# Taking the first expert's first 128 rows out of the expert stage and into the last steps of attention

## The chip, the cores and the metric

The kernel runs on one core of a Trainium2 chip. The metric is the device time of one execution in microseconds (us). A matmul engine (TensorE, PE in the rows; its weight loads are PEld), a vector engine (VectorE, DVE), an activation engine (ScalarE, ACT), a general engine (GpSimd, POOL) and a queue engine that mostly starts transfers (SyncE, SP) run in parallel, each in its own program order, and wait for one another through semaphores. A name with a q behind it (PEldq, DVEq, SPq) is the sequencer of that engine.

## The reference

Three layers, one after the other:

```
scores = q @ k.T / 8            # 4 batches, 8 heads, 576 tokens, 64 wide
keep the 32 largest scores of each row, softmax over them, times v
x = heads side by side          # 2304 tokens x 512
rows with x @ w_skip > 0:  e = argmax(x @ w_gate)      # 8 experts
    x += gate * (relu(x @ w1[e]) @ w2[e])              # w1 512x1024, w2 1024x512
h = x @ w_in;  g = h * sigmoid(1.702 h);  out = g @ w_out   # 512 -> 2048 -> 512
```

All weights are given, all in float32 except w_in and w_out, which come as float64. Counted from the reference's inputs, expert 0 gets 26, 31, 48 and 26 rows in the four batches (131 in all) and expert 1 gets 62; the largest expert has 182.

## The kernel before

**Attention.** `body` runs a loop over steps n = 0, 1, 2, ... Each step holds one block of 128 query rows of one head, nine blocks to a pair of heads, 16 pairs, so NTL = 144 blocks. A block passes through some twenty small stages, each delayed by a fixed number of steps: scores on TensorE (`qk`), copy (`scopy`), search for the 32nd largest on VectorE (`cand`, `merge`, `below`, `pick`), masks on ScalarE and GpSimd (`sign`, `side`, `center`, `clip`), transposes on TensorE (`tpose`, L370 and L371), exponentials (`evac`, L359) and the product with v (`av`, L427 to L434). The lists `stages` and, from step 146, `tail` set the order in which a step's instructions enter the queues. The loop ends with n = 157; from n = 144 on no new block begins and the pipeline runs empty.

**Routing.** After each batch the gates are computed and every row gets a place in its expert's list: `rank` (matmuls), `place` (VectorE and GpSimd), `lists` (five matmuls, L703, and an addition to LST, L706). For batch 3, the last, this is the way into the next stage: `last_gate` (L547 to L553) adds the last heads' share of the gates block by block, `gating_last` and `rank` run behind the loop, then `place`, `order` (which puts the experts in order of size, expert 0 always first), `short_lists` (L716), a gather of the first expert's rows (`first_rows`, L117) and a branch (L927 reads a flag, L1008 is the branch) past code for rows that do not fit. Short runs of matmuls that compute nothing (`warm`, L259) stand around `rank`.

**Experts.** Eight experts in the order `turns`. The four largest have room for 192 rows (a tile of 128 and one of 64), the others for 128. `turn` (L1078) transposes the gathered rows, `layer1` (L1091) multiplies with w1 in plain fp32, `layer2` (L1109) multiplies with w2 split in two fp32r parts (`split_w2`, L1136 and L1137): 24 matmuls of 512 columns for a tile of 128 rows, 16 for one of 64. In the same loop SP loads w1 two experts ahead (L94; two buffers) and w2 one ahead (L104), and `split_f64` turns the float64 w_in into two fp32r parts, in 16 chunks (L1030 the load, L1033 to L1035 on VectorE, L1038 and L1039). `take(e)` starts the chunks that expert e converts after its layer 1: three for a large expert, one for a small one. The last expert's chunk is converted inside its layer 1, at f = 2. Results go back to memory by an indirect write (`scatter`, L1126).

**The last layer** is a dense loop of fp32r matmuls that ends the kernel, and no line of the change is in it.

Of the kernel before, what the change touches and what calls it, by code (L numbers as in the profile page):

```python
# [8 lines left out]
F32 = mybir.dt.float32  # L9
F32R = mybir.dt.float32r  # L10
BF16 = mybir.dt.bfloat16
I32 = mybir.dt.int32
# [17 lines left out]
def body(ctx: ExitStack, tc: tile.TileContext, q, k, v, w_skip, w_gate, w1, w2, w_in, w_out, out):  # L30
    nc = tc.nc
    V, A, G, T, SY = nc.vector, nc.scalar, nc.gpsimd, nc.tensor, nc.sync
    P = 128
# [77 lines left out]
    V.tensor_copy(own, iop)  # L111
    IX0 = cst.tile([P, 2], I32, name="IX0")
    IXG = cst.tile([P, 2], I32, name="IXG")
    ZD = dram.tile([P, 8], F32, name="ZD")

    def fetch_rows(xg, ix, src=XD):
# [4 lines left out]
    def first_rows(ready=False):  # L121
        w, src = (DM, X2D) if ready else (DM + 1, XD)
        if not ready:
            V.tensor_copy(IX0, IDX[:, :2])
            gate_places()
        fetch_rows(x0[0][:, :w], IX0[:, :1], src)
        fetch_rows(x0[1][: NS - P, :w], IX0[: NS - P, 1:], src)

    def gate_places():
        V.tensor_scalar(IXG, IX0, float(DM + 1), float(DM), op0=ALU.mult, op1=ALU.add)  # L130

    def first_gates():
        one = XD.rearrange("r (w o) -> (r w) o", o=1)
        fetch_rows(x0[0][:, DM:], IXG[:, :1], one)
        fetch_rows(x0[1][: NS - P, DM:], IXG[: NS - P, 1:], one)

    with ExitStack() as ph:
        ph.enter_context(tc.manual_schedule())
# [399 lines left out]
        def last_gate(r, u):  # L538
            b, hp = divmod(NP - 1, HP)
            xb, g = xbs[b % 2], gs_[b % 2]  # L540
            rows = P if r < 4 else 64
            if r == 0 and u == 0:
                st["lx"] = wp.tile([P, S], F32, name="z")
            xt = st["lx"][:, r * P : r * P + rows]
            zt, zg = SS[:, r * P : r * P + rows], SS[:rows, 1024 + 9 * r : 1033 + 9 * r]
            if u == 0:
                T.transpose(zt, xb[:rows, r, hp * P : (hp + 1) * P], ident[:rows, :rows])  # L547
            elif u == 1:
                V.tensor_copy(xt, zt)
            elif u == 2:  # L550
                T.matmul(zg, xt, W9[:, hp, :], start=True, stop=True)
            else:
                V.tensor_tensor(g[:rows, r, :], g[:rows, r, :], zg, op=ALU.add)  # L553
            yield
# [193 lines left out]
        def stage(f, m):  # L748
            yield from f(m) or ()
# [21 lines left out]
        G.iota(tie, pattern=[[-1, E]], base=0, channel_multiplier=0, allow_small_or_imprecise_dtypes=True)  # L771
        A.activation(tie, tie, AF.Copy, scale=1.0 / 16)
        V.memset(tie[:, :1], 1.0e6)
        place_no = xbp.tile([P, E, E], F32, name="place_no")
        G.iota(place_no, pattern=[[1, E], [0, E]], base=0, channel_multiplier=0, allow_small_or_imprecise_dtypes=True)
        expert_no = xbp.tile([1, E, E], F32, name="expert_no")
# [5 lines left out]
        by_place = least[:, : 2 * E * E].rearrange("p (a c e) -> p a c e", a=E, c=2)  # L782
        over = xbp.tile([1, E], F32, name="over")
        kept = xbp.tile([1, E, E], F32, name="kept")

        def order():
            V.tensor_tensor(rnk, base, tie, op=ALU.add)
# [64 lines left out]
        V.tensor_copy(IOF.rearrange("p (e c) -> p e c", c=2), ior[:, :LW].rearrange("p (e c) -> p e c", c=NTT)[:, :, :2])  # L852
        V.tensor_copy(WHICH, which)
        fetch_rows(x0[0][:, :8], own, ZD)
        CHECKS = [NTL + AVL - 4, NTL + AVL - 2, NTL + AVL + 3]
        for n in range(NTL + AVL + 4):
            p, i = divmod(n, 9)
# [4 lines left out]
            if n == NTL // 2:  # L862
                w1t = load_w1(0)
                raws = load_w2(0)
            live = [stage(f, n - lag) for f, lag in (tail if n >= NTL + LAST else stages) if span(f, n - lag)]
            gates = [(p - 2, i - 6) if i >= 6 else (p - 3, i + 3)]
            gates = [gu for gu in gates if 0 <= gu[0] < NP - 1]
# [9 lines left out]
            if i == 0 and "fin" in st:  # L877
                todo.append(place())
                fresh.append(todo[-1])
            elif i == 0 and "hot" in st:  # L880
                live.append(lists(1))
            live += [some(g, 3 if g in fresh or n >= NTL else 1) for g in todo]
            fresh.clear()
            while live:
                live = [g for g in live if next(g, 1) is None]
# [9 lines left out]
                    next(last_gate(r, 2 * w))  # L895
            if n in CHECKS:
                check(CHECKS.index(n))
            if i == 8 and "fin" in st:
                rank()
            elif i == 8 and "hot" in st:  # L900
                next(lists(0))
        for g in todo:
            for _ in g:
                pass
        warm(2)
        rank()
        warm(7)
        pg, og = place(), order()
        next(pg)
        next(pg)  # L910
        for w, _ in enumerate(pg):
# [4 lines left out]
            if 1 < w < 5:  # L916
                next(og, None)
        short_lists(0)
        short_lists(1)
        first_rows(True)  # L920
        for _ in og:
# [2 lines left out]
        st.pop("hot")  # L924
        sort_lists()
        gate_places()
        fine = nc.values_load(flags[:, 1:2], min_val=0, max_val=1)  # L927

        def exact(n):
# [78 lines left out]
        with tc.If(fine < 1):  # L1008
            full_lists()
            good = nc.values_load(flags[:, :1], min_val=0, max_val=1)  # L1010
            with tc.If(good < 1):
                for t in (base, LST):
                    V.memset(t, 0.0)
                with tc.For_i(0, B, 1) as bv:
                    again(bv)
            V.tensor_scalar(IDX, LST, padf, None, op0=ALU.add)
# [42 lines left out]
    with ExitStack() as ph:  # L1059
# [25 lines left out]

        def layer1(w1t, xgT, ns, step):
            hb = mp.tile([P, FC1, 2 * NS], F32R, name="hb", bufs=1)
            for f in range(FC1):
# [3 lines left out]
                A.activation(hb[:, f, :ns], ph_[:, :ns], AF.Relu)  # L1092
                for a, b in ((0, 2 * P), (P, NS))[: 1 + (ns > P)]:
                    V.scalar_tensor_tensor(hb[:, f, b : b + min(P, ns - a)], ph_[:, a : min(a + P, ns)], 0.0,  # L1094
                                           hb[:, f, a : min(a + P, ns)].bitcast(F32), op0=ALU.max, op1=ALU.subtract)
                step(f)
            return hb

# [28 lines left out]
                out=X2D, out_offset=bass.IndirectOffsetOnAxis(ap=ix, axis=0), in_=xo, in_offset=None,  # L1127
            )

        late = []  # L1130
        spare = []

        def split_w2(raws, ws, f, long):
# [11 lines left out]
                todo.append(split_f64(wt, w_in[c * P : (c + 1) * P, us], wih[:, c, us], wil[:, c, us],  # L1145
                                      SY if c or u > 2 else A))

        turns = [0, 4, 1, 5, 2, 3, 6, 7]
        slots = []
        for k in turns:  # L1150
            slots.append([(IXS[:, k, :1], P)] + ([(IXS[: NS - P, k, 1:], NS - P)] if k < BIGS else []))
        who = [0]
        for k in turns[1:]:
            who.append(nc.values_load(flags[:, 2 + E + k : 3 + E + k], engines=[mybir.EngineType.SP], min_val=0, max_val=E - 1))
        nxt = []
        xgs = x0
        nx = turn(slots[0], xgs)
        first_gates()
        def take(e):
            gs = [todo.pop(0) for _ in range(3 if turns[e] < BIGS else 1)]  # L1160
            for g in gs:
                next(g)
            return gs

        w1s = [w1t, load_w1(who[1])]
        ahead = take(0)
        nxt.append(gather(slots[1]))
        for e in range(E):
            long = turns[e] < BIGS
            ns = NS if long else P  # L1170
            ws = ([], [])

            def step(f):
# [183 lines left out]
```

## Time and profile before

| | us |
|---|---|
| three runs | 1033.44, 1039.68 (median), 1041.09 |
| profiled execution | 1033.63, its span 1030.7 |
| TensorE busy / weight loads | 989.4 / 842.9 |
| VectorE / ScalarE / GpSimd busy | 704.6 / 593.1 / 478.3 |
| mean granted TensorE clock | 0.988 of full |

A row of the view by windows gives, for a stretch in us from the span's start, the busy time of each engine, how many instructions began, the granted TensorE clock (1.00 is 2.4 GHz, 0.50 is 1.2 GHz), the busy share of the 16 transfer engines and what they moved in GB/s. The chain of waits is followed backwards from the last instruction: each line is a start, a length and what the kernel's end hung on then. A timeline line is a start, a length, engine, line, operation, tiles and count; in brackets the idle time of the engine before it and what ended that. A fp32 matmul appears as two records, a fp32r one as one.

Attention takes the span's first 455 us, the experts the stretch from 467 to 615 us, the last layer the rest.

### The profile page before, as it was taken

The numbers are of one execution on the slowest core, as the hardware profiler recorded it, in microseconds if no ns is written. First come the engines' busy times: TensorE is split into PE (matmuls) and PEld (weight loads), VectorE is DVE, ScalarE is ACT, GpSimd is POOL, SyncE is SP. The second block draws the span as 40 slices with busy tenths as digits, with TensorE's granted clock in tenths as the row PEclk, the third lists the DMA queues.
The fourth block names the chain that finished last, engine by engine and source line by source line (L and its number), as shares of the span: only waits on it lengthen the run. The fifth ranks groups of instructions, "written<-read, shape, count | busy, mean of one in ns | idle before, by whom it ended". The sixth has DMA issues, their size and how long they took to land.

```text
span 1030.7 us, 20024 instructions
## 1 busy us (share of the span) xinstructions
PE 989.4 (96%) x6499; PEld 842.9 (82%) x6499; DVE 704.6 (68%) x3326; ACT 593.1 (58%) x1261; POOL 478.3 (46%) x598
## 2 busy tenths in 40 slices
PE   7999999999999999878999989999999999999998
PEld 4888888888888888757989877888888888888887
DVE  7999999999999999965898976653232323322222
ACT  6999999999999999823534533332222222222222
POOL 5788888978898879733765652220000000000000
PEclk9999999999999999998999999999999999999999
DMA  3121116161511151037889863312000200100000
GB/s 87 44 45 38 33 37 130 40 203 40 132 40 40 40 125 24 1 95 281 276 328 385 301 218 134 102 62 73 10 1 1 82 1 1 62 1 1 9 33 21
DMA packets 99010, 92.11 MB, mean 89 GB/s; under 512 B 71760, under 2 KB 71760, under 8 KB 98896
## 3 DMA queue, kind: packets, MB, share of 16 engines
q1 hardware_dynamic: 96704, 83.91, 26.8%
q0 software_dynamic: 1760, 5.25, 1.5%
q10 hardware_dynamic: 432, 1.57, 0.4%
q8 instruction: 53, 0.87, 0.4%
q14 instruction: 61, 0.50, 0.2%
HBM read 72.38 MB, written 17.32 MB: 87 GB/s over the span
## 4 chain that ended last, share of the span: by engine, by line
PE 71%; DVE 18%; DMA 4%; ACT 3%; issue 2%; POOL 1%; another core or an unknown queue 1%; SPq 0%; DVEq 0%; ACTq 0%; POOLq 0%
PE ph L1279 19%; PE py L1264 18%; PE Y L430 7%; DVE C L296 5%; PE SS L273 5%; PE pt L370 4%; DVE z L329 2%; DMA raw<-in_moe_w_in_dram 2%; PE ph L1091 2%; PE pt L371 2%; PE SS L275 2%; PE py L1109 2%; DVE w2l L1137 1%; PE Y L427 1%; PE SS L267 1%
## 5 line engine op out<-in xcount | busy, mean ns | idle before, releaser
L296 DVE MAX8 C<-s 128x8 f32<-128x72 f32 x1152 | 222.0, 220 | 2.2 <-ACT s L289 2.2
L324 POOL TENSOR_TENSOR z<-s,z 128x576 f32<-128x576 f32 x144 | 203.3, 1412 | 43.3 <-ACT z L319 41.1
L1267 DVE TENSOR_TENSOR g<-py,g 128x512 f32<-128x512 f32 (+1 forms) x80 | 51.1, 639 | 180.1 <-ACT g L1266 180.1
L1266 ACT ACTIVATE g<-py 128x512 f32<-128x512 f32 (+1 forms) x80 | 44.3, 554 | 166.9 <-PE py L1264 166.8
L430 PE MATMUL Y<-vn,AT 128*128 128x65 f32 x1024 | 121.3, 272 | 0.0
L430 PEld LDWEIGHTS Y<-vn,AT 128*128 128x128 f32 x1024 | 119.4, 192 | 0.0
L356 ACT ACTIVATE k<-s,th 128x576 bf16<-128x576 f32 x144 | 113.4, 788 | 5.6 <-DVE T L337 5.0
L1279 PE MATMUL ph<-woh,gh 128*128 128x512 f32 x288 | 112.6, 391 | 3.3 <-ACT gh L1269 3.3
L319 ACT ACTIVATE z<-s,T 128x576 f32<-128x576 f32 x144 | 113.0, 785 | 4.0 <-DVE T L312 1.8
L370 PE MATMUL pt<-ident,a 128*128 128x128 f32 x576 | 114.6, 279 | 0.8 <-issue 0.8
L1279 PE MATMUL ph<-woh,gl 128*128 128x512 f32 x288 | 112.5, 391 | 0.0
L1279 PE MATMUL ph<-wol,gh 128*128 128x512 f32 x288 | 112.5, 391 | 0.0
L351 POOL TENSOR_SCALAR a<-s,m 128x576 f32<-128x576 f32 x144 | 108.0, 750 | 1.5
L329 DVE MAX8 z<-z 128x8 f32<-128x576 f32 x144 | 107.0, 743 | 0.2 <-POOL z L324 0.2
L371 PE MATMUL pt<-far,k 128*128 128x128 bf16 x576 | 106.1, 220 | 0.6 <-ACT k L356 0.5
L359 ACT ACTIVATE AT<-pt 128x512 f32<-128x512 f32 x144 | 86.7, 602 | 8.5 <-PE Y L430 7.2
L370 PEld LDWEIGHTS pt<-ident,a 128*128 128x128 f32 x576 | 82.9, 144 | 6.3 <-issue 1.0
L1271 DVE TENSOR_TENSOR gl<-g,gh 128x512 fp32r<-128x512 f32 (+1 forms) x80 | 51.1, 639 | 52.4 <-ACT gh L1269 48.5
L1264 PE MATMUL py<-xh,wih 128*128 128x512 f32 (+1 forms) x320 | 81.1, 375 | 0.8 <-ACT xh L1298 0.8
L1091 PE MATMUL ph<-xgT,w1t 128*128 128x192 f32 (+1 forms) x512 | 75.8, 309 | 6.1 <-DVE hb L1094 5.4
L1091 PEld LDWEIGHTS ph<-xgT,w1t 128*128 128x128 f32 x512 | 74.1, 197 | 7.8 <-DVE hb L1094 6.5
L1269 ACT ACTIVATE gh<-g 128x512 fp32r<-128x512 f32 (+1 forms) x80 | 47.1, 589 | 56.6 <-DVE g L1267 56.6
(263 smaller groups left out, 2137.1 us busy)
## 6 DMA issues: line engine op xcount, KB each, us to landing
w1t<-in_moe_w_dram SPq DMA_DIRECT2D x8, 2048.0 KB
w<-in_moe_w_dram SPq DMA_DIRECT2D x64, 256.0 KB
raw<-in_moe_w_out_dram SPq DMA_DIRECT2D x16, 512.0 KB
raw<-in_moe_w_in_dram SPq DMA_DIRECT2D x13, 512.0 KB
out_dram<-ot SPq DMA_DIRECT2D x18, 256.0 KB
qn<-in_q_dram SPq DMA_DIRECT2D x32, 128.0 KB
kn<-in_k_dram SPq DMA_DIRECT2D x32, 128.0 KB
vn<-in_v_dram SPq DMA_DIRECT2D x32, 128.0 KB
```

What stands on the lines that cost most here:

```text
L296: V.max(C[:, g, :], s[:, g * SEG : (g + 1) * SEG])
L319: A.activation(z, d["s", c], AF.Sign, bias=T24[:, NTL + 6 - n : NTL + 7 - n], scale=-1.0 - 2.0 ** -20, accum_out=sg)
L324: G.tensor_tensor(z, d["s", c], z, op=ALU.mult)
L329: V.max(z8, d.pop(("z", c)))
L351: G.tensor_scalar(a[:, o : o + S], d.pop(("s", c)), -1.0, d.pop(("m1", c))[:, :1], op0=ALU.mult, op1=ALU.add)
L356: A.activation(d["k", r][:, o : o + S], d["s", c], AF.Relu, bias=d.pop(("th", c)), scale=-1.0)
L370: T.matmul(out, a, ident, is_transpose=True, start=True, stop=False)
L371: T.matmul(out, d["k", r][:, sl], far, start=False, stop=True)
L430: T.matmul(y[:, w * j : w * j + w], t[:, 4 * j + g, :], d["v"][:, g, j, :], start=False, stop=(j == 1 and g == 3))
L1091: T.matmul(ph_[:, :ns], w1t[:, c, f * P : (f + 1) * P], xgT[:, c, :ns], start=(c == 0), stop=(c == KC - 1))
L1264: T.matmul(phh[:, :n], lh[:, c, fs], rh[:, c, :n], start=(u == 0 and c == 0), stop=(u == 2 and c == KC - 1))
L1279: T.matmul(po[t], lh[:, ts_], rh[f], start=(f == 0 and u == 0), stop=(f == FC2 - 1 and u == 2))
```

## The change

The first 128 places of expert 0 are filled from batches 0 to 2 alone: after those batches' lists, `base` of expert 0 is raised to at least 128, so that the last batch's rows begin at place 128. The rows are gathered on their own (`early_rows`), and `early_turn` computes them in plain fp32, in 20 slices that enter the queues at the end of steps 148 to 157 (table `EARLY`) and behind the loop, in place of the `warm` matmuls. After the branch expert 0 has one tile of 64 rows. The early result is added by `early_out` just ahead of the branch and is the first to be scattered.

Around this: the lists of batch 2 are made earlier (two pieces of `place` a step from step 135, and its lists as soon as `place` is through instead of at a pair's end), expert 1 is forced to the last place in the order of sizes and is always computed second, so that its w1 can be loaded in attention (step 90) instead of after the branch; `turns` and the chunks of w_in per expert (`MORE`) change; `last_gate` uses other columns of the buffer SS, whose third part the early work takes.

```diff
-        fetch_rows(x0[0][:, :w], IX0[:, :1], src)
         fetch_rows(x0[1][: NS - P, :w], IX0[: NS - P, 1:], src)
...
+        V.memset(tie[:, 1:2], -1.0e6)
...
+        def early_rows():
+            V.tensor_scalar(base[:, :1], base[:, :1], float(P), None, op0=ALU.max)
+            V.tensor_scalar(IXA, LST[:, :1], padf, None, op0=ALU.add)
+            V.tensor_scalar(IXB, LST[:, :1], padf, float((B - 1) * S - 1), op0=ALU.add, op1=ALU.min)
+            fetch_rows(x0[0], IXB, XD[: (B - 1) * S, :])
+            yield
+        EZ = SS[:, 1024:]
+        def early_turn():
+            for c in range(KC):
+                T.transpose(EZ[:, c * P : (c + 1) * P], x0[0][:, c * P : (c + 1) * P], ident)
+            yield
+            st["ex"] = sp.tile([P, 2, S], F32, name="s").rearrange("p j k -> p (j k)")
+            A.activation(st["ex"][:, :DM], EZ, AF.Copy)
+            st["eh"] = sp.tile([P, 2, S], F32, name="s").rearrange("p j k -> p (j k)")
+            yield
+            for f in range(FC1):
+                z = EZ[:, f % 4 * P : (f % 4 + 1) * P]
+                for c in range(KC):
+                    T.matmul(z, w1t[:, c, f * P : (f + 1) * P], st["ex"][:, c * P : (c + 1) * P],
+                             start=(c == 0), stop=(c == KC - 1))
+                yield
+                if f % 4 == 3:
+                    A.activation(st["eh"][:, (f - 3) * P : (f + 1) * P], EZ, AF.Relu)
+                    yield
+            for f in range(FC1):
+                T.matmul(EZ, st["eh"][:, f * P : (f + 1) * P], raws[f], start=(f == 0), stop=(f == FC1 - 1))
+                yield
+        def early_out():
+            V.scalar_tensor_tensor(x0[0][:, :DM], EZ, x0[0][:, DM:], x0[0][:, :DM], op0=ALU.mult, op1=ALU.add)
...
+        SOON = NTL - 9
+        EARLY = {4: 1, 5: 1, 6: 1, 7: 1, 8: 2, 9: 2, 10: 1, 11: 2, 12: 1, 13: 1}
...
+            if n == NTL * 5 // 8:
+                w1u = load_w1(1)
...
-            elif i == 0 and "hot" in st:
+            elif st.pop("listed", i == 0 and n < SOON and "hot" in st):
                 live.append(lists(1))
-            live += [some(g, 3 if g in fresh or n >= NTL else 1) for g in todo]
+                if n > SOON:
+                    live.append(early_rows())
+            live += [some(g, 3 if g in fresh or n >= NTL + 4 else 2 if n >= SOON else 1) for g in todo]
...
+            for _ in range(EARLY.get(n - NTL, 0)):
+                next(eg, None)
...
-        warm(2)
+        next(eg)
         rank()
-        warm(7)
+        for _ in range(4):
+            next(eg)
...
         short_lists(0)
+        for _ in eg:
+            pass
         short_lists(1)
...
         gate_places()
+        early_out()
...
-        late = []
+        late = [(IXA, x0[0][:, :DM])]
...
-        turns = [0, 4, 1, 5, 2, 3, 6, 7]
+        turns = [0, E - 1, 1, 4, 2, 3, 5, 6]
+        MORE = [1, 2, 3, 2, 3, 3, 2, 0]
...
+        slots[0] = slots[0][1:]
...
-            gs = [todo.pop(0) for _ in range(3 if turns[e] < BIGS else 1)]
+            gs = [todo.pop(0) for _ in range(MORE[e])]
...
-        w1s = [w1t, load_w1(who[1])]
+        w1s = [w1t, w1u]
...
-            long = turns[e] < BIGS
-            ns = NS if long else P
+            long = 0 < e and turns[e] < BIGS
+            ns = NS if long else P if e else NS - P
```

## Rows read from the trace of the kernel before

**Rows 1.** View by windows, stretches of 5 us: four near attention's end, one among experts.
```profile
425.00:430.00 5.00, 4.11 (x39) 3.59 (x38) 5.00 (x36) 3.65 (x10) 3.86 (x6) 1.00 0.01 3
...
440.00:445.00 5.00, 3.54 (x35) 3.28 (x33) 3.02 (x9) 2.46 (x5) 3.29 (x7) 1.00 0.01 3
445.00:450.00 5.00, 5.00 (x47) 4.63 (x46) 3.08 (x14) 1.15 (x3) 0.00 (x0) 1.00 0.00 0
450.00:455.00 5.00, 3.92 (x28) 3.17 (x28) 2.63 (x14) 0.38 (x1) 0.00 (x0) 1.00 0.65 235
...
475.00:480.00 5.00, 5.00 (x33) 5.00 (x32) 2.94 (x10) 3.20 (x9) 1.94 (x2) 1.00 1.01 384
```

**Rows 2.** The chain of waits, from the last gates to the branch.
```profile
441.66 0.39 PE SS L551 x2
...
446.67 1.73 PE Y L430 x16
...
449.90 0.51 PE Z L703 x5
...
454.45 0.30 PE SS L551 x2
...
456.13 0.21 DVE MS L617
...
459.67 0.20 DVE hc L683
...
461.59 5.57 another core or an unknown queue
```

**Rows 3.** Timeline of TensorE in the expert loop.
```profile
467.30 1.70 PE L1078 MATMUL pt<-ident,xg 128*128 128x128 f32 x8 [5.71 <-remote]
469.60 12.66 PE L1091 MATMUL ph<-xgT,w1t 128*128 128x192 f32 x64 [0.60 <-ACT xgT L1080]
...
482.45 0.48 PE L1109 MATMUL py<-w2h,hb 128*128 128x512 f32 x1
...
491.62 7.70 PE L1091 MATMUL ph<-xgT,w1t 128*128 128x128 f32 x64
...
505.65 10.56 PE L1091 MATMUL ph<-xgT,w1t 128*128 128x192 f32 x64
...
606.89 2.08 PE L1091 MATMUL ph<-xgT,w1t 128*128 128x128 f32 x8 [3.45 <-DVE hb L1094]
```

**Rows 4.** Timelines of single instructions whose like the change adds or removes.
```profile
446.19 0.60 ACT L359 ACTIVATE AT<-pt 128x512 f32<-128x512 f32 x1 [0.91 <-PE pt L371]
...
450.87 0.30 DVE L706 TENSOR_TENSOR LST<-LST,Z 128x144 f32<-128x144 f32 x1 [0.64 <-ACT xt L522]
...
462.15 1.11 POOL L117 DMA_INDIRECT xg<-X2D,IX  x1 [1.25 <-DVE kept L809]
...
463.14 0.16 DVE L130 TENSOR_SCALAR IXG<-IX 128x2 int32<-128x2 int32 x1
...
602.17 0.43 DVE L1033 TENSOR_SCALAR t<-raw 128x512 int32<-128x512 int32 x1 [1.15 <-DMA raw<-in_moe_w_in_dram]
```

**Rows 5.** Transfers into the tile xg, from issue to landing, stretch 440 to 520.
```profile
DMA to landing us min/median/max: 3.3/5.8/6.9
```

**Rows 6.** The branch's line L1008: its instructions on two sequencers (duration in ns).
```profile
L1008 PEldq COMPARE_BRANCH  x1: 4007/4007/4007, 462.0 to 462.0; - x1
...
L1008 DVEq EVENT_SEMAPHORE  x2: 21/21/21, 467.0 to 467.1; - x2
```

**Rows 7.** View by windows of 1 us; the granted clock is third from the end.
```profile
457.00:458.00 1.00, 1.00 (x4) 0.33 (x3) 0.96 (x10) 0.00 (x0) 0.14 (x1) 0.50 1.08 225
...
464.00:465.00 1.00, 0.00 (x0) 0.00 (x0) 0.00 (x0) 0.00 (x0) 0.48 (x1) 0.50 0.74 209
...
472.00:473.00 1.00, 1.00 (x5) 1.00 (x5) 0.07 (x1) 0.43 (x2) 0.00 (x0) 0.50 0.92 336
...
474.00:475.00 1.00, 1.00 (x8) 1.00 (x8) 0.14 (x1) 0.50 (x2) 0.77 (x1) 1.00 1.01 398
```

More of the change, by code (lines that the diff above doesn't have):

```diff
@@ L113, in body @@
     IXG = cst.tile([P, 2], I32, name="IXG")
+    IXA = cst.tile([P, 1], I32, name="IXA")
+    IXB = cst.tile([P, 1], I32, name="IXB")
     ZD = dram.tile([P, 8], F32, name="ZD")
@@ L132, in first_gates @@
     def first_gates():
-        one = XD.rearrange("r (w o) -> (r w) o", o=1)
-        fetch_rows(x0[0][:, DM:], IXG[:, :1], one)
-        fetch_rows(x0[1][: NS - P, DM:], IXG[: NS - P, 1:], one)
+        fetch_rows(x0[1][: NS - P, DM:], IXG[: NS - P, 1:], XD.rearrange("r (w o) -> (r w) o", o=1))
     with ExitStack() as ph:
@@ L544, in last_gate @@
             xt = st["lx"][:, r * P : r * P + rows]
-            zt, zg = SS[:, r * P : r * P + rows], SS[:rows, 1024 + 9 * r : 1033 + 9 * r]
+            z0 = r % 4 * P
+            zt, zg = SS[:, z0 : z0 + rows], SS[:rows, 512 + 9 * r : 521 + 9 * r]
             if u == 0:
@@ L897, in body @@
                 check(CHECKS.index(n))
+            for _ in range(EARLY.get(n - NTL, 0)):
+                next(eg, None)
             if i == 8 and "fin" in st:
                 rank()
-            elif i == 8 and "hot" in st:
+            elif "hot" in st and (i == 8 if n < SOON else i != 5 and "listed" not in st):
                 next(lists(0))
+                if n >= SOON:
+                    st["listed"] = True
         for g in todo:
@@ L1015, in body @@
                     again(bv)
+                V.tensor_copy(IXA, padf)
+                V.tensor_scalar(IDX, LST, padf, None, op0=ALU.add)
+                spill(0, 0)
             V.tensor_scalar(IDX, LST, padf, None, op0=ALU.add)
@@ L1087, in layer1 @@
             hb = mp.tile([P, FC1, 2 * NS], F32R, name="hb", bufs=1)
+            spans = [(0, ns, P, NS)] if ns < P else [(0, P, 0, 2 * P), (P, ns, P, NS)][: 1 + (ns > P)]
+            o = spans[0][2]
             for f in range(FC1):
@@ L1091, in layer1 @@
                     T.matmul(ph_[:, :ns], w1t[:, c, f * P : (f + 1) * P], xgT[:, c, :ns], start=(c == 0), stop=(c == KC - 1))
[L1092 to L1095, printed above, removed]
+                A.activation(hb[:, f, o : o + ns], ph_[:, :ns], AF.Relu)
+                for a, b, hi, lo in spans:
+                    V.scalar_tensor_tensor(hb[:, f, lo : lo + b - a], ph_[:, a:b], 0.0,
+                                           hb[:, f, hi : hi + b - a].bitcast(F32), op0=ALU.max, op1=ALU.subtract)
                 step(f)
@@ L1151, in body @@
             slots.append([(IXS[:, k, :1], P)] + ([(IXS[: NS - P, k, 1:], NS - P)] if k < BIGS else []))
-        who = [0]
-        for k in turns[1:]:
+        slots[0] = slots[0][1:]
+        who = [0, 1]
+        for k in turns[2:]:
             who.append(nc.values_load(flags[:, 2 + E + k : 3 + E + k], engines=[mybir.EngineType.SP], min_val=0, max_val=E - 1))
         nxt = []
-        xgs = x0
+        xgs = x0[1:]
         nx = turn(slots[0], xgs)
```

1 line of the change is left out of this document (added).

## The prediction

> **What bounds the kernel now.** I read the view by windows first: it shows which engine is full in which stretch. Up to step 147 VectorE has no pause (5.00 of 5 in 425 to 430 us) and TensorE has some. From 441.7 us it is the other way: in 445 to 450 TensorE is busy 5.00 of 5 with its weight loads at 4.63, while VectorE has 3.08 [rows 1]. The chain of waits says the same in order of time: it lies on TensorE's queue from 441.66 until the last product with v, crosses to VectorE for the last gates (454.45 to 456.34), through `rank` and `place` to the first operand of the short lists at 459.87, and then 5.57 us stand to a queue the view can't name [rows 2]. Line L1008 names it: TensorE's branch took 4.0 us, and VectorE came out of its own at 467.0 [rows 6]. After that TensorE is the bound: expert 0 fills it from 467.30 to 491.62 [rows 3]. So the change adds TensorE work in a stretch where TensorE is short of time, and takes it out of another such stretch. The forecast is the difference.
>
> **What is added ahead of the branch.** A slice of layer 1 is 4 matmuls, 8 records of 128 columns at 7.70 / 64 = 0.120 us: 0.96 us [rows 3]. A slice of layer 2 is one fp32 matmul of 512 columns, which no row shows. By columns it costs 10.56 / 64 x 512 / 192 = 0.44 us a record, 0.88 a slice; from the step between 128 and 192 columns it is 0.40 and 0.79 [rows 3]. I take 0.87, near the first, since the pace there is set by columns. In the order of the queue:
>
> - The transposes (step 148) and their copy by ScalarE (0.60 [rows 4]) cost nothing: TensorE has 1.46 us to spare in 440 to 445 [rows 1], just ahead of 441.66, where it waits for VectorE. Without that cover: 0.7.
> - f = 0 to 3 (steps 150 to 152) stand in TensorE's queue ahead of the last two products with v: 4 x 0.96 = 3.8. The lists of batch 2, five matmuls on the chain here, leave: -0.5 [rows 2]. f = 4 writes where the relu of the first four is still reading, so TensorE waits for a copy of 0.60 [rows 4], with the last product with v queued behind it: +0.6; then itself, +1.0. Together +4.9.
> - f = 5 falls into the pause before the last gates (TensorE has 1.08 of 5 to spare in 450 to 455 [rows 1]): +0.1. f = 6 and 7 stand ahead of the last gate's matmul, 1.9 against some 0.4 of that pause: +1.5.
> - The second relu, 0.6, and two slices of layer 2, 1.7, come ahead of `rank`, beside the gating chain from the last gate to MS, 456.34 - 454.75 = 1.6 [rows 2]: +0.7.
> - Four more slices, 3.5, lie between `rank` and the short lists, where VectorE takes until 459.87 [rows 2]: nothing, if the clock is full. The last two, 1.7, run in the branch's wait.
> - `early_out` stands in VectorE's queue ahead of its branch and waits for those two slices; TensorE waits for VectorE's way out of the branch [rows 6]. I take +0.5, between 0 (the sequencers run ahead) and 2.3 (two slices and a pass like the copy of 0.60, if all queue up), nearer to the first, as TensorE's branch began at 462.0, right behind the last list matmul's end at 461.59 [rows 2, 6]. The gather of 128 rows that leaves (POOL, 1.11 [rows 4]) gives nothing back: the smaller one has its place and the branch outlasts it. The Trainium skill, Runtime: NRT & Kernel Launch, section Instruction fetch mechanics, says that a taken branch out of the fetched pages stalls its engine for a fetch; by that rule the 4.0 us begin only once the queue has come to the branch, and the sum would be up to 1.2 us higher. The trace agrees as to the 4.0 us [rows 6]; where they begin behind queued matmuls it doesn't show.
> - VectorE gets three small operations of 0.16 and the addition to LST, 0.30, earlier [rows 4], all where it is full: +0.8. The other work of `place` moves by a few steps within that stretch: nothing. GpSimd's gather, 1.1, meets an engine with 1.1 of 5 idle [rows 1]; without that cover 1.1. It lands within 6.9 us [rows 5], issued near 430 and wanted near 439.
>
> Sum: 4.9 + 0.1 + 1.5 + 0.7 + 0.5 + 0.8 = **+8.5 us**, bounds 3 to 12.
>
> **What leaves behind the branch.** Before, 24.3 us pass from 467.30 to 491.62. After: one set of transposes and one copy of the two, 1.3 instead of 2.3 [rows 3]. Layer 1 with 64 columns: its nearest rows are the 65-column records of L430, 1.73 / 16 = 0.108 [rows 2], so 64 x 0.108 = 6.9. The clock is at 1.2 GHz after the wait, 0.50 from 464 to 473 and 1.00 at 474 [rows 7]; that cost layer 1 12.66 - 10.56 = 2.1 us [rows 3], and I leave it: 9.0 (6.9 if the clock holds, 10.5 if weights load at half pace as well). Next expert's transposes 0.2. Layer 2: 16 matmuls instead of 40 at (491.62 - 482.45) / 40 = 0.229: 3.7. Together 14.2: **-10.1**.
>
> The last expert no longer converts a chunk. Before, that chunk's wait for its load (1.15 on VectorE at 602.17 [rows 4]) stopped TensorE for 3.45 at 606.89 [rows 3]. Now the expert before it has two chunks, which delays its successor's first relu by some 0.4: **-3.0**. The second and fourth experts get a second chunk too; with transfers full (1.01 at 475 to 480 [rows 1]) I take **+0.5**, bounds 0 to 7. The load of w1, 2 MB, that moves into attention is issued in step 90, seven steps ahead of SP's next transfers, and costs nothing; without that cover up to a step, 455 / 158 = 2.9.
>
> Sum: 8.5 - 10.1 - 3.0 + 0.5 = **-4.1 us**. The profiled execution, 1033.6, would become 1029.5. The median run lies 6.1 above it; the mean of the three is 1038.1, and from that I say **1034**.
>
> **The rivals.**
>
> *The early slices find more room than I count.* From 440 to 455 weight loads leave 1.72 + 0.37 + 1.83 = 3.9 of 15 us free [rows 1]; if the slices used all of it, f = 0 to 7 (7.7) would cost 7.7 - 3.9 - 0.5 = 3.3 instead of 6.5: -7.3, 1031. If the clock also held after the branch, -9.4, 1029. Against it: the records of L430 follow each other at 0.108 us, without pause [rows 2]. The Trainium skill, Perfetto Trace Analysis, section Identifying the Most-Contended Engine, says that matmul busy time is a poor measure and weight-load busy share the better one; by that rule 445 to 450 is 93% full rather than 100%, and the first figure above is its sum. The trace agrees for that stretch within 0.4 us; whether the other room can be used it doesn't show. Chance 0.20.
>
> *Slower: the second chunk stops TensorE.* In the second, fourth and seventh expert a chunk more stands in VectorE's queue ahead of the next expert's relu. Where its load lands after the layer 2 it hides behind, TensorE stops as at 606.89. Price: 3 x 3.45 = 10.4 in place of 0.5: +5.8, 1044. It decides where the second load of a pair lands later than the layer 2 in which it hides, 24 x 0.229 = 5.5 us. For it: transfers are full from 475 on; against: w1's 2 MB less are asked for. Chance 0.13.
>
> *The clock is low in the late slices.* At 457 it was 0.50 [rows 7], after a stretch with pauses. At 1.2 GHz the slices around `rank` cost 1.7 + 3.5 + 1.7 more: +2.8, 1041. Against: the slices fill those very pauses. Chance 0.10.
>
> *It doesn't do what it says*, because rows don't fit: expert 0 has 105 rows in three batches and 26 in the last, against 128 and 64, and expert 1 has 62 against 128. Excluded but for oversights: 0.02.
>
> **How the numbers follow.** The forecast as summed, between -9 and +3, has 0.55. About 1%, 10.4 us, is what a measurement can tell from no change. Beyond it on the fast side lie 0.10 of the forecast, 0.11 of the first rival, 0.01 of the rest: 0.22. On the slow side 0.02, 0.06, 0.03 and 0.01: 0.12. Within: 0.66. The range runs from -10.4 on the fastest run to a little over +2 on the slowest: 1023 to 1043.
>
> **What would show it.** Right: `rank` near 464 instead of 456.4; TensorE without pause from 441 to there; 14 to 15 us between the first transposes after the branch and the second expert's layer 1; no stop in the last expert's layer 1; a clock of 1.00 up to the branch. Wrong: `rank` before 461 (the slices found room), stops of over 1 us in the third, fifth or eighth expert, or a late landing of the early rows, which would hold TensorE's whole queue from step 148.

## The result and the profile after

The changed kernel takes 1046.7 us in the median of 11 runs (1043.7 to 1050.4), the kernel before 1035.7 in as many beside it: ratio 1.0101, 95% interval 1.0072 to 1.0129. It is slower by 1%, some 10.5 us, where I had forecast 4 us faster. The profiled execution took 1045.8 us, its span 1043.9.

The starts of a few instructions cut the spans into stages. Beside before and after stands a kernel from the experiments below, the changed one with a single line moved (f2_after_gather, here f2); its trace has the same mean clock as that of before, 0.988, while that of the changed kernel has 0.978. Block 143 is the last block of attention; a block is taken at the start of its MAX8 over 576 columns on VectorE. What I call the restart is the first transposes behind the branch.

| stage, us | before | after | f2 | forecast for after |
|---|---|---|---|---|
| start to block 133 | 411.7 | 413.9 | 413.2 | 411.7 |
| block 133 to block 143 | 29.0 | 31.7 | 29.7 | 29.8 |
| block 143 to `rank` | 15.7 | 26.2 | 25.2 | 22.9 |
| `rank` to the restart | 10.9 | 11.0 | 10.8 | 11.4 |
| expert 0 | 24.3 | 20.3 | 20.1 | 14.2 |
| second expert | 14.0 | 17.4 | 13.6 | - |
| third expert's layer 1 to the end | 525.1 | 523.4 | 519.8 | - |
| the last two together | 539.1 | 540.8 | 533.4 | 536.6 |
| span | 1030.7 | 1043.9 | 1032.4 | 1026.6 |

The timeline of TensorE after answers to [rows 3]:

```profile
471.81 0.25 PE L634 MATMUL Z<-MS,upper 128*128 128x48 bf16 x1
...
482.86 0.43 PE L1130 MATMUL pt<-ident,xg 64*128 64x64 f32 x4 [3.96 <-DVEq L1057]
483.97 13.91 PE L1145 MATMUL ph<-xgT,w1t 128*128 128x64 f32 x64 [0.67 <-DVE xgT L1134]
497.68 1.06 PE L1130 MATMUL pt<-ident,xg 128*128 128x128 f32 x4
...
503.16 7.31 PE L1145 MATMUL ph<-xgT,w1t 128*128 128x128 f32 x64
511.94 0.63 PE L1130 MATMUL pt<-ident,xg 128*128 128x128 f32 x4 [1.47 <-DMA xg<-XD,IXS]
...
568.15 1.33 PE L1130 MATMUL pt<-ident,xg 128*128 128x128 f32 x8 [2.84 <-DMA xg<-XD,IXS]
...
618.99 3.86 PE L1145 MATMUL ph<-xgT,w1t 128*128 128x128 f32 x32 [1.24 <-DVE hb L1148]
```

Three things are to be seen. Expert 0's layer 1, with 64 columns, takes 13.91 us, more than the 12.66 it took with 192. TensorE then stops at the transposes of the third expert's gathered rows, for 1.47 us, and at 568.15 at those of the sixth, for 2.84. The list of TensorE's waits (us in all, times, longest) has 4.7 us of them in place of 0.8. The last expert's stop has shrunk from 3.45 to 1.24. Before, and after:

```profile
PE pt L1078 <- DMA xg<-XD,IXS: 0.8, 2, 0.4
```

```profile
PE pt L1130 <- DMA xg<-XD,IXS: 4.7, 3, 2.8
...
PE ph L1145 <- DVE hb L1148: 1.2, 1, 1.2
```

The windows after, as in [rows 1] and [rows 7]:

```profile
428.00:436.00 8.00, 8.00 (x48) 7.34 (x47) 6.87 (x46) 5.74 (x15) 4.32 (x4) 0.57 0.13 35
...
450.00:455.00 5.00, 5.00 (x49) 4.92 (x47) 2.31 (x9) 0.84 (x2) 0.00 (x0) 1.00 0.00 0
...
484.00:500.00 16.00, 16.00 (x72) 15.71 (x73) 5.18 (x14) 5.93 (x16) 7.62 (x7) 0.50 0.62 173
513.00:518.00 5.00, 5.00 (x18) 3.91 (x19) 4.90 (x13) 0.74 (x2) 0.00 (x0) 0.66 0.78 235
```

Throughout expert 0's layer 1 the clock is at 0.50, and behind the stop at 511.94 it has fallen again. The chain of waits of this trace has no piece ahead of 600 us, so nothing answers to [rows 2].

Why the rows come late stands on GpSimd's queue. After:

```profile
497.03 1.27 POOL L1191 TENSOR_TENSOR w2l<-w,w2h 128x512 fp32r<-128x512 f32 x1 [2.15 <-ACT w2h L1190]
502.52 1.28 POOL L1091 TENSOR_TENSOR wil<-t,wih 128x512 fp32r<-128x512 f32 x1 [4.22 <-ACT wih L1090]
503.95 0.98 POOL L119 DMA_INDIRECT xg<-XD,IXS  x1
505.24 1.00 POOL L119 DMA_INDIRECT xg<-XD,IXS  x1 [0.30 <-issue]
```

And VectorE's instructions that this subtraction waits for:

```profile
499.30 0.68 DVE L1134 COPY xgT<-pt 128x512 f32<-128x512 f32 x1
499.90 0.42 DVE L1085 TENSOR_SCALAR t<-raw 128x512 int32<-128x512 int32 x1
500.36 0.69 DVE L1086 SCALAR_TENSOR_TENSOR t<-raw,t 128x512 int32<-128x512 int32 x1
501.08 0.69 DVE L1087 SCALAR_TENSOR_TENSOR t<-raw,t 128x512 int32<-128x512 int32 x1
```

The gather of the next expert but one (L119) is queued behind the chunk of w_in that an expert converts. GpSimd stands idle for 4.22 us before that chunk's subtraction, and the rows land up to 7.9 us after their issue (3.6/4.1/7.9 are the least, median and most of the tile's landings from 478 to 520 us, in place of [rows 5]).

So a chain begins at the end of expert 0's layer 1 that a faster layer 1 does not shorten: transposes and copy (497.88 to 499.98), conversion on VectorE (to 501.77), ScalarE and GpSimd (to 503.80), then the gathers, the first issued at 503.95 and landed at 511.9: 14.0 us. Beside it TensorE has layer 2 and the next layer 1. Before, that was 499.16 - 482.26 = 16.9 us, from the end of layer 1 to the third expert's transposes, which began without a stop. TensorE and GpSimd before:

```profile
499.16 0.99 PE L1078 MATMUL pt<-ident,xg 128*128 128x128 f32 x8
```

```profile
493.96 1.46 POOL L117 DMA_INDIRECT xg<-XD,IXS  x1 [0.15 <-issue]
495.72 1.29 POOL L117 DMA_INDIRECT xg<-XD,IXS  x1 [0.30 <-issue]
```

Behind three chunks the second gather left 13.5 us after the end of layer 1. With the least landing of [rows 5], 3.3, that makes an estimate of 16.8 us for this chain: it was nearly level with TensorE, and the 0.8 us of waits, two of 0.41 at the fifth and the sixth expert, say the same of the later ones. The change takes 24 of 40 matmuls out of expert 0's layer 2 and only two chunks out of the chain. With TensorE's part at full clock, 0.4 + 16 x 0.23 + 7.3 = 11.4 us, a stop of some 2.6 would have followed however fast layer 1 had become.

### The profile page after: what moved, and what is told of

The parts are those of the page before. It is cut to its first block, busy times and chain, and to the rows that moved or that the text cites. A ratio compares the mean times of both kernels' runs of the same rounds, so it can differ in the third digit from the quotient of the medians.

```text
span 1043.9 us, 20094 instructions
## 1 busy us (share of the span) xinstructions
PE 1005.3 (96%) x6546; PEld 853.4 (82%) x6546; DVE 700.6 (67%) x3321; ACT 593.8 (57%) x1263; POOL 476.6 (46%) x598
## 5 line engine op out<-in xcount | busy, mean ns | idle before, releaser
L369 PE MATMUL pt<-ident,a 128*128 128x128 f32 x576 | 116.9, 283 | 0.0
L370 PE MATMUL pt<-far,k 128*128 128x128 bf16 x576 | 108.2, 222 | 0.5 <-ACT k L355 0.3
L358 ACT ACTIVATE AT<-pt 128x512 f32<-128x512 f32 x144 | 86.7, 602 | 11.6 <-PE Y L429 7.3
L1320 PE MATMUL py<-xh,wil 128*128 128x512 f32 (+1 forms) x320 | 78.9, 368 | 0.0
L1320 PE MATMUL py<-xl,wih 128*128 128x512 f32 (+1 forms) x320 | 78.8, 368 | 0.0
## 6 DMA issues: line engine op xcount, KB each, us to landing
raw<-in_moe_w_in_dram SPq DMA_DIRECT2D x13, 512.0 KB, 10.9
```

The lines of the kernel that those rows point to most:

```text
L358: A.activation(o, i, AF.Exp, scale=-UNSC)
L369: T.matmul(out, a, ident, is_transpose=True, start=True, stop=False)
L370: T.matmul(out, d["k", r][:, sl], far, start=False, stop=True)
L1320: T.matmul(phh[:, :n], lh[:, c, fs], rh[:, c, :n], start=(u == 0 and c == 0), stop=(u == 2 and c == KC - 1))
```

## The experiments

**Does the narrow layer 1 keep the clock low, or the wait at the branch? (e1_wide)**

```diff
                     V.tensor_copy(xgT[:, :, :rows], pt[:, :, :rows])
+                    if rows < P:
+                        A.activation(xgT[:, :, rows : 2 * rows], pt[:, :, :rows], AF.Copy)
```

(That is in `turn`; in the matmul of `layer1` the columns `: ns` become `: max(ns, P)`.)

> The changed kernel, with expert 0's 64 remaining rows put twice side by side, so that its layer 1 behind the branch runs 128 columns instead of 64 (the second half is not used). Theory: the 64-column layer 1, whose matmuls are as short as the loads of their weights, leaves TensorE at 1.2 GHz; with 128 columns the clock comes back within some 7 us of the restart, as it did in the kernel before, and the 64 records take about 64 x 0.120 + 2.1 = 9.8 us, at most 11, instead of 13.9: 3 to 4 us off the changed kernel's time although there are twice the columns. Rival: the clock is low because of the idle wait at the branch, whatever the width; the 64 records then stand at the half-clock pitch all the way, 13.7 us or more, and nothing is gained. Second rival: it is no clock matter, the loads of weights alone set 0.214 us a record; then also 13.7 or more, with the granted clock at 1.00 in that stretch.

Measured: 1.0069 (1.0036 to 1.0102; such figures are the ratio to the kernel before and its 95% interval). That is 3.3 us below the changed kernel, in the theory's 3 to 4, though the two intervals overlap. Layer 1 with twice the columns took 9.45 us instead of 13.91. Its windows:

```profile
480.00:482.00 2.00, 2.00 (x9) 2.00 (x10) 0.00 (x0) 0.00 (x0) 0.80 (x1) 0.50 0.49 88
482.00:484.00 2.00, 2.00 (x11) 2.00 (x10) 0.23 (x1) 0.92 (x4) 1.06 (x1) 0.50 0.77 295
484.00:486.00 2.00, 2.00 (x18) 2.00 (x18) 1.07 (x3) 1.39 (x5) 1.38 (x3) 0.92 0.17 64
486.00:488.00 2.00, 2.00 (x20) 2.00 (x20) 1.39 (x4) 1.70 (x6) 1.49 (x2) 1.00 0.77 290
...
506.00:514.00 8.00, 8.00 (x27) 6.31 (x27) 5.99 (x10) 1.65 (x3) 2.58 (x2) 0.65 0.96 310
```

At the restart, at 478.25, the clock has fallen to 0.50, and 7 us later it is back. Only the columns differ, so the wait at the branch alone did not keep the clock low; and the second rival wanted 1.00 where the changed kernel has 0.50 (484 to 500 us above). But in this trace the second expert takes 21.0 us instead of 17.4: TensorE waits 2.9 us for the third expert's rows and then works at a low clock (506 to 514). From the restart to the end the kernel needs 561.9 us, and the changed one needs 561.0. In the traces, then, what the faster layer 1 gave was lost one expert later; the 3.3 us by the runs these stages do not show.

**Is it the early pacing? (e2_pace)**

```diff
-            live += [some(g, 3 if g in fresh or n >= NTL else 1) for g in todo]
+            live += [some(g, 3 if g in fresh or n >= NTL + 4 else 2 if n >= SOON else 1) for g in todo]
...
```

(That is in the kernel before; the lists of batch 2 come as soon as `place` is through.)

> The kernel before with nothing but the changed pacing: place and the lists of batch 2 are begun and stepped earlier in attention's last nine steps; no early rows, no slices, the old order of experts. Theory: the pacing alone, by putting VectorE's work into steps where VectorE is full, stops TensorE near step 139 and lets its clock fall, and costs some 3 us up to step 143, less the five list matmuls that leave the end (0.5): ratio about 1.002 to 1.003, the MAX8 of block 143 near 444 instead of 440.7 us, and a granted clock under 0.9 in some window between 424 and 436. Rival: the pacing is free and the early gather and its three small operations stop TensorE there: ratio 1.000, block 143 at 440.7, clock as before.

Measured: 1.0009 (0.9977 to 1.0042), which decides between neither. Its trace has block 143 at 446.0 and the clock at 0.50 from 428 to 436. But the paced kernels whose clock is full there (e1, e7 and f2) take only 0.7 us more than before between blocks 133 and 143. I put pacing and early gather together at that.

**The order of the experts alone (e3_order)**

```diff
+        V.memset(tie[:, 1:2], -1.0e6)
+            if n == NTL * 5 // 8:
+                w1u = load_w1(1)
-        turns = [0, 4, 1, 5, 2, 3, 6, 7]
+        turns = [0, E - 1, 1, 4, 2, 3, 5, 6]
+        MORE = [1, 2, 3, 2, 3, 3, 2, 0]
```

> The kernel before with nothing but the changed order behind the branch: expert 1 put last in rank and second in turn, its w1 loaded during attention, the order of sizes and the number of chunks split in each expert (1, 2, 3, 2, 3, 3, 2, 0) as in the changed kernel; expert 0 whole behind the branch, nothing early. Theory (as forecast): the last expert's stop of 3.45 goes and the extra chunks cost 0.5: -3 us, ratio 0.997. Rival: the extra chunks, the transfers that they ask for and the gathers behind them stop TensorE in the second and fifth expert, as the changed kernel's trace has it (1.5 and 3.2 us): +1 to +3 us, ratio 1.001 to 1.003.

Measured: 0.9977 (0.9950 to 1.0005), -2.4 us: near the theory's number, though not parted from no change. The rival's mechanism is in the trace as well: 3.4 us of waits for gathered rows in place of 0.8, against 3.8 us less of waits for relu, the last expert's above all. Its trace shows one thing more, told under the hardware below.

**The early slices (e4_noslices)**

```diff
-        EARLY = {4: 1, 5: 1, 6: 1, 7: 1, 8: 2, 9: 2, 10: 1, 11: 2, 12: 1, 13: 1}
+        EARLY = {}
...
```

(`warm(2)` and `warm(7)` stand around `rank` again, and `early_out` is gone: the first 128 rows of expert 0 get no expert output.)

> The changed kernel without the early expert work (its 20 slices of transposes, layer 1 and layer 2 and the addition at the end are left out, so the first 128 rows of expert 0 get no expert output), with the filler matmuls around rank put back; early gather, pacing, order and the 64-row expert 0 stay. Theory: the slices cost some 10 us between step 143 and rank and nothing else; rank comes at 456.4 + 3.3 (pacing) = 459.7, and expert 0 behind the branch is no shorter than with them, some 20 us, as the clock stays at 1.2 GHz there all the same: 10 us off the changed kernel, ratio about 1.000. Rival: the slices in the branch's wait are what keeps the clock low behind it, or what is late at the restart; without them expert 0 takes 14 to 15 us as forecast and the ratio is about 0.994.

Measured: 0.9942 (0.9908 to 0.9976). Expert 0 was no shorter, 20.6 us with the clock at 0.50 through its layer 1, as the theory had it; but the ratio is the rival's. By the runs leaving the slices out is worth some 16 us, against 10.5 between block 143 and `rank` in the traces. The profiled run here was its slowest of ten (1038.5, median 1031.7), with block 143 only at 448.0, so its stages can't tell where the other 5 come from. That stays open.

**Work in the branch's wait (e5_bridge, e6_before_bridge)**

```diff
         for _ in eg:
             pass
+        warm(18)
         short_lists(1)
```

(This is e5, filler matmuls in the changed kernel; e6 puts `warm(24)` at the same place in the kernel before.)

> The changed kernel with 18 filler matmuls of 512 columns behind the last slice of layer 2, so that TensorE has work during the branch (18 x 0.21 = 3.9 us at full clock, against 3.9 us from the last slice to the restart). It tells whether 64-column matmuls can hold a clock that is up already, where e1_wide showed that 128 columns raise one that is down. Theory A (64 columns neither raise nor hold it): the clock is at 1.00 at the restart, falls within layer 1, and layer 1 takes 11 to 13.9 us; ratio 1.007 to 1.010. Theory B (they can't raise it but hold it): layer 1 at 1.00 throughout, 64 x 0.108 = 7 us instead of 13.9, expert 0 in 13 to 14 us instead of 20.3; but the third expert's rows, whose gather waits on GpSimd behind a chunk's subtraction, come no earlier than about 26 us after the restart, and so only some 3 of the 6 to 7 us show in the total: ratio about 1.007. If the filler ran at half clock it would last 7.7 us and delay the restart by 3.8.

> The kernel before with 24 filler matmuls of 512 columns behind the list matmuls, 24 x 0.21 = 5.0 us at full clock against the 5.7 us of the branch. Theory: the clock is at 1.00 at the restart, expert 0's transposes and layer 1 take 1.5 and 10.6 us instead of 2.3 and 12.7, and the second expert's layer 1 comes 2 to 3 us earlier after the restart; the third expert's gather lands then about as late as TensorE wants it, which takes back up to 2: -1 to -3 us, ratio 0.997 to 0.999. Rival: the clock at the list matmuls is low more often than not, the filler lasts up to 10 us and the restart is up to 4 us late: ratio 1.001 to 1.003.

e5: 1.0138 (1.0121 to 1.0155), slower than either theory had it; the profiled run was its fastest of five (1042.0, median 1048.5), so the trace does not tell why. The clock was up at the restart, at 480.67, and fell all the same:

```profile
480.00:482.00 2.00, 0.66 (x6) 0.55 (x7) 0.42 (x1) 0.00 (x0) 1.70 (x2) 1.00 0.27 72
482.00:484.00 2.00, 1.54 (x11) 1.51 (x11) 0.07 (x1) 0.33 (x2) 0.08 (x1) 0.69 0.81 283
484.00:496.00 12.00, 12.00 (x59) 12.00 (x59) 3.75 (x11) 5.30 (x15) 6.08 (x5) 0.50 0.52 163
```

So theory A in the trace: layer 1 with 64 columns ran at 0.50 to its end even from a full clock, 13.8 us. The fall itself can't be put down to the columns: TensorE was busy for only 0.66 of the 2 us after 480, and in e6 the clock falls behind the restart with 192 columns. e6: 0.9974 (0.9941 to 1.0007), within the theory's range but not parted from no change. In its trace the clock falls from 475 on and is back at 479 under 192 columns; the second expert's layer 1 comes 23.3 us after the restart instead of 24.3, but the restart 13.0 us after `rank` instead of 10.9.

**The gather's place (e7_gather, f2_after_gather, f1_order_gather)**, the same edit in three kernels: e1, the changed one and e3.

```diff
+            if e + 2 < E:
+                nxt.append(gather(slots[e + 2]))
             for g in convs:
                 next(g)
                 next(g)
-            if e + 2 < E:
-                nxt.append(gather(slots[e + 2]))
```

> The kernel of e1_wide (64 rows put twice, 128 columns) with one more edit: the gather of the next but one expert's rows is issued ahead of the conversion of the chunks instead of behind it, on GpSimd's queue. Theory: in e1_wide what a faster expert 0 gave was lost in the second expert, because its successor's rows were fetched behind a subtraction that waits for a chunk's load; the second expert took 21.0 us instead of 14. With the gather ahead the rows lie there in time, TensorE does not stop at the third expert's transposes (2.1 and 0.8 us in e1_wide), the clock stays up in the layer 2 that follows, the second expert takes 14 to 16 us, and the fifth expert's wait of 3.2 us goes too: 6 to 9 us off e1_wide, ratio 0.998 to 1.001. Rival: the wait is for the transfers themselves (w1 and w2 in front of the rows), and the gather, issued earlier, lands as late as before: ratio 1.006 to 1.008.

> The changed kernel with the gather ahead of the chunks and nothing else. Theory: what the gather's place costs does not depend on the columns of layer 1; as between e1_wide and e7_gather it gives back most of 9 us even though expert 0 stays at half clock: -5 to -9 us against the changed kernel, ratio 1.002 to 1.006, with no wait for gathered rows and the second expert back at 14 us. Rival: with expert 0 at half clock the rows were late by only 1.5 us at the third expert and 2.8 at the sixth, so no more than 4.7 us come back: ratio 1.006 to 1.009.

> e3_order (the kernel before with only the changed order of experts) and the gather ahead of the chunks. Theory: the order by itself was worth 2.4 us because its gathers, behind a chunk's subtraction on GpSimd, stopped TensorE for 3.4 us in all, and the clock fell after the longest of these stops; without them it gives 5 to 8 us: ratio 0.992 to 0.995, and no wait for gathered rows in TensorE's list. Rival: only the 3.4 us of TensorE's waits come back, or less, since relu and conversions on VectorE are the next bound: ratio 0.995 to 0.998.

e7: 0.9979 (0.9948 to 1.0011), 9.3 us below e1. f2: 1.0001 (0.9970 to 1.0033): the moved line alone gives back 10 us, the whole loss, more than the theory's 5 to 9 and twice the waits that it removes. f1: 0.9955 (0.9924 to 0.9986), 2.3 us below e3, which is the rival's range and within both intervals. No wait for rows is left in any of the three. GpSimd and TensorE in f2, the last line from TensorE's waits:

```profile
493.27 1.27 POOL L1191 TENSOR_TENSOR w2l<-w,w2h 128x512 fp32r<-128x512 f32 x1 [2.14 <-ACT w2h L1190]
494.69 0.99 POOL L119 DMA_INDIRECT xg<-XD,IXS  x1
495.99 0.92 POOL L119 DMA_INDIRECT xg<-XD,IXS  x1 [0.30 <-issue]
498.76 1.27 POOL L1091 TENSOR_TENSOR wil<-t,wih 128x512 fp32r<-128x512 f32 x1 [1.86 <-ACT wih L1090]
```

```profile
480.21 13.91 PE L1145 MATMUL ph<-xgT,w1t 128*128 128x64 f32 x64 [0.67 <-DVE xgT L1134]
...
498.94 7.31 PE L1145 MATMUL ph<-xgT,w1t 128*128 128x128 f32 x64
506.08 0.99 PE L1130 MATMUL pt<-ident,xg 128*128 128x128 f32 x8
...
512.56 10.56 PE L1145 MATMUL ph<-xgT,w1t 128*128 128x192 f32 x64
```

```profile
PE ph L1145 <- DVE hb L1148: 3.6, 3, 1.9
```

The gathers leave 0.6 us after the end of expert 0's layer 1 (494.12) instead of 6.1 (497.88 to 503.95). The transposes at 506.08 follow layer 1 without a stop, the layer 2 behind them runs at full clock, and from the restart to the end the kernel needs 553.5 us instead of 561.0. Of those 7.5 us TensorE is idle for 2.6 less (4.7 less of waits for rows, but 2.4 more for relu) and busy for 5.0 less, in part the half clock behind the two stops. The other 2.5 of the 10 I can't place: the two traces differ ahead of the branch by 4.0 us, with the clock at 0.57 from 428 to 436 in one and at 1.00 in the other.

The runs show the clock's part as well. Their mean granted clock is 0.980 in the changed kernel and 0.985 in f2, 0.985 in e1 and 0.990 in e7; if the 0.9 us for each 0.001 found below hold there, some 4 us of either gain go with the clock, and the remaining 6 and 5 are near the waits removed, 4.7 and 5.7. In e3 and f1, alike at 0.983, the line gives 2.3. That the moved line raises the clock is seen only behind its stops, not shown for all of the 4 us.

**The slices where TensorE waits (e8_late, f3_late_wide)**

```diff
-        EARLY = {4: 1, 5: 1, 6: 1, 7: 1, 8: 2, 9: 2, 10: 1, 11: 2, 12: 1, 13: 1}
+        EARLY = {4: 1, 5: 1}
-        next(eg)
         rank()
...
```

(In the changed kernel; `early_out` stands behind the branch, and the gather is moved as above; f3 is also widened as e1.)

> The changed kernel with the early slices put where TensorE waits anyway: transposes and copy at steps 148 and 149 as they were, none in the last steps of attention or ahead of rank, layer 1's f = 0 to 3 between rank and the short lists, the other 14 slices in the wait of the branch, the addition at the end behind the branch instead of ahead of it; and the gather ahead of the chunks as in e7_gather. Theory: the slices cost 10 us where they stood because TensorE is full from block 143 to rank; here rank comes 15.7 to 16.5 us after block 143, as before, the remaining slices take 12 us at full clock from the list matmuls on, of which the branch hides 5.7, so the restart is some 17 us after rank (10.9 before); the clock is up at the restart, and expert 0's rest takes 14 to 15 us. Against the kernel before: +0.6 (pacing) + 6.3 - 9.5 - 2.4 (order) = -5, ratio about 0.995. Rival: VectorE leaves the branch only when the slices are done, the restart is 4 us later still, and the clock falls in between: ratio 1.000 to 1.004.

> e8_late with the 64 rows put twice, so that layer 1 behind the branch has 128 columns as in e1_wide. Theory: expert 0's layer 1 falls from 13.4 to 9.3 us or less, and as the gathers are no longer late the 4 us reach the total: ratio 0.997 to 0.998, and the clock comes back within some 6 us of the restart. Rival: the late slices take so long that the restart is the loss, and the next expert's relu or its chunks take back what layer 1 gives: ratio 1.000 to 1.002.

e8: 1.0015 (0.9990 to 1.0040), the rival's range. `rank` came 16.1 us after block 143, as expected, but the restart 19.2 after `rank` instead of 17, in part since TensorE waited for the addition (1.25 us ahead of its transposes), and layer 1 again took 13.6 us, at half clock from 483 on. f3: 0.9976 (0.9944 to 1.0008), the theory's range, though neither parted from no change nor clear of e8: layer 1 down by 4.7 us, of which 2.8 stay to the end in the trace and 4.0 by the runs.

**Without any early work (f4_order_gather_bridge)**: the kernel before with e3's order, the gather ahead, and `warm(20)` behind its list matmuls.

> f1_order_gather with 20 filler matmuls behind the list matmuls, as in e6_before_bridge: the candidate to beat both kernels without any of the early work. Theory: the 2.7 us of e6 and what f1 gives add up: 2 to 3 us off f1, ratio 0.990 to 0.993, expert 0's layer 1 at or soon back at full clock. Rival: the clock falls at the restart all the same, as it did in e6's own trace at 475 us, and the filler gives 0 to 1 us: the same ratio as f1.

Measured: 0.9917 (0.9883 to 0.9950), the theory's range, 1026.5 us in the median of 12: it beats both kernels. It lies 3.9 us below f1, whose interval overlaps with its own. In the trace the clock held through the restart, at 467.67:

```profile
466.00:468.00 2.00, 1.33 (x8) 0.63 (x7) 0.00 (x0) 0.00 (x0) 0.00 (x0) 1.00 0.06 16
468.00:470.00 2.00, 1.40 (x11) 1.10 (x10) 0.69 (x1) 0.38 (x1) 1.08 (x2) 1.00 0.00 0
470.00:472.00 2.00, 2.00 (x15) 2.00 (x14) 0.42 (x2) 0.85 (x2) 1.70 (x2) 1.00 0.71 211
```

Layer 1 of 192 columns took 10.67 us instead of 12.66.

## Why the prediction was wrong

**What bounds the kernel** was read rightly up to the branch: TensorE is nearly full from block 143 to `rank`, and what is added there is paid.

**Ahead of the branch, +8.5 forecast.** In f2, at the clock of before, the restart comes 11.6 us later. The slices cost 9.5 of that instead of 7.2 (by the runs of e4 it may be more). The rows of f2 that split it:

```profile
458.06 1.06 PE L432 MATMUL pt<-vn,AT 128*128 128x130 f32 x8
...
464.38 0.28 PE L551 MATMUL SS<-W,z 128*64 128x9 f32 x2 [0.39 <-DVE z L549]
466.29 1.96 PE L814 MATMUL SS<-w,s 128*128 128x512 f32 x4 [1.62 <-ACT ex L610]
468.08 0.19 PE L634 MATMUL Z<-MS,upper 128*128 128x48 bf16 x1
```

From block 143 to the last products with v it is 15.2 us against 9.9: +5.3, forecast 4.9. From there to the last gate's matmul 6.3 against 3.9: +2.4, forecast 1.6. From there to `rank` 3.7 against 1.9: +1.8, forecast 0.7, since the two slices of layer 2 start 1.6 us late and only then run, 1.8, ahead of `rank`. Pacing and small operations gave +0.7 (forecast 0.8). The last 1.5 arose ahead of block 133 and are not the change's: 1.1 of them are there at block 9 (43.3 us against 42.2), and the ten blocks from 90 on, where w1 is now loaded, take 29.5 us in both. So the change's own part is +10.1. The first rival, that the slices find room, fails on the same rows: the weight loads are busy 4.92 of 5 in 450 to 455.

**The branch, +0.5**, came to nothing: 10.8 against 10.9. TensorE's branch began at 477.4 and took 3812 ns, near the 4007 of [rows 6], while its slices still ran to 478.90:

```profile
L1057 PEldq COMPARE_BRANCH  x1: 3812/3812/3812, 477.4 to 477.4; - x1
```

```profile
476.94 1.96 PE L814 MATMUL SS<-w,s 128*128 128x512 f32 x4
```

The branch ran beside the queued matmuls, so the 1.2 us that I had set apart for the other case did not come. The Trainium skill, Runtime: NRT & Kernel Launch, section Instruction fetch mechanics, has a taken branch to a target outside the fetched pages stall its engine for a fetch. The 3.8 us agree with that; that a fetch is what they are, no run here shows.

**Behind the branch, -10.1: the step that failed.** It failed twice. First its size: I let the clock come back after 2.1 us' worth of loss, as it had with 192 columns in [rows 3]; with 64 it stayed at 0.50 to the end of the layer, 13.9 us instead of 9.0. That is twice the 6.9 of my full clock and beyond my bound of 10.5. In the changed kernel the clock was still up at the restart and fell some 0.6 us later, just ahead of layer 1; in e5 and e8 it fell some 2 us after the restart, within layer 1; and in e1, with 128 columns, it came back though it was down at the restart. Where the gather is moved, the wide layer 1 is worth 2.3 us by the runs (e7 against f2) and 4.0 (f3 against e8), neither clear of the intervals. Second, and worse, it took what leaves expert 0 as gone from the end. I had counted what stands ahead of TensorE, not what the next expert but one waits for: the chain on VectorE and GpSimd that ends with its rows was nearly level with TensorE before. From the restart to the end I had forecast 12.6 us less than before, with the terms below. The changed kernel needs 2.4 less, and e1, whose layer 1 is 4.5 us shorter, 1.5 less in its trace; with the gather moved, in f2, it is 9.9 less.

**The extra chunks, +0.5 with bounds 0 to 7, and the second rival.** The term was the other half of the same mistake. I asked what is queued behind a second chunk on VectorE, the next relu, and not on GpSimd, where the gather stands behind every chunk's subtraction. The second and fourth experts got a second chunk each, and behind the fourth's the sixth expert's rows were 2.84 us late. The rival had the right sign and the wrong queue: 1044 for stops at the relu, chance 0.13.

**The last expert, -3.0**: its stop fell from 3.45 to 1.24, a gain of 2.2; e3 has -2.4 for the whole order, not parted from nothing.

**Summed:** forecast -4.1, measured +10.5 by the runs, a miss of 14.6. The gather's place is 10.4 of it by f2, with what the clock has in that. The 4.2 that are left are in f2's trace: 10.1 - 8.5 = 1.6 ahead of the branch and 12.6 - 9.9 = 2.7 behind it, where expert 0 took 5.9 longer than forecast and the others 3.2 less. **The third rival**, a low clock in the slices around `rank`, is in the trace after (`rank` waited for two slices that took 2.97 us, at 0.50 from 470 on) but not in that of f2 (1.96 us), and moved `rank` by 1 us.

## What to carry to other kernels

When work is taken off the bounding engine, look for what the next stages wait for, queue by queue, and ask how much earlier it could come; a wait of 0.4 us that is there already can mean that a second chain is level with the first. An instruction that starts a transfer belongs ahead of any conversion in its engine's queue that waits for other data. A matmul shape narrower than any in the trace should be priced at both levels of the clock, for the whole of its stretch.

## What the runs showed of the hardware

**Single executions differ by more than the change, and the clock goes with it.** Over the 35 runs of the kernel before that stood beside the last experiments, the time falls by 0.9 us for each 0.001 of mean granted clock (correlation -0.88), from 1030 us at 0.988 to 1044 at 0.973 to 0.975. The same instructions can lie in a half-clock stretch in one trace and not in the next. Between block 143 and `rank` e3 changes nothing; e3 first, then before:

```profile
443.00:460.00 17.00, 17.00 (x80) 15.44 (x79) 5.02 (x22) 1.53 (x4) 0.00 (x0) 0.50 0.16 62
```

```profile
443.00:460.00 17.00, 14.52 (x106) 10.87 (x104) 10.77 (x62) 2.18 (x6) 1.32 (x4) 0.90 0.49 140
```

The restart came 7.4 us later in e3's trace, and by its runs e3 is no slower a kernel. So stages of two traces are compared only where the clocks agree, and the sum is left to the runs.

**Where the clock came back.** In the five traces with 64 columns in layer 1 (after, f2, e4, e5, e8) the clock was at 0.50 from its first 2 us to its end; behind it, in layer 2 with its 512 columns, 1.00 came back after some 2 to 4 us. In the traces with 128 or 192 columns in that place it was back within layer 1, or had not fallen (f4).
